# Staging the last weight through three buffers, and the front of a seven-product stage, in a three-layer kernel on one core

## The chip, the cores and the metric

The kernel runs on one core of one Trainium2 chip. The metric is the device time of one execution in microseconds; the median of three executions before the change is 565.75 us (564.25 to 565.76). Five engines matter, each with a queue of its own that is worked off in order: TensorE (PE), VectorE (DVE), ScalarE (ACT), GpSimd (POOL) and SyncE (SP), which here only starts transfers.

## What is computed

```python
x = attention(q, k, v)        # 2 x 8 heads, 768 positions, head size 64: a window of +-15
                              # positions and one summary (max of k, mean of v) per 32 positions
x = x.transpose(0, 2, 1, 3).reshape(1536, 512)
a, b = x @ w1, x @ w2         # 512 -> 1024
x = ((a * b) @ w3) @ w_out    # 1024 -> 1024 -> 512
h = x @ w_in                  # 512 -> 2048
g = h * clip(h + 3, 0, 6) / 6
out = g @ moe2_w_out          # 2048 -> 512
```

The weights are float64 and reach the chip as pairs of 32-bit words. All large products are made in float32 quality: each operand is held as a rounded part and a remainder, and a product of two such operands is three matmuls.

## The kernel before, in words

The 1536 rows are three blocks of 512. A slot of the arena holds one 128 x 512 tile as its two parts (1024 words a partition). PE first multiplies w3 and w_out into one weight W', then for each block forms a and b from w1 and w2 (16 tiles, the middle weights), the gated tile a * b, and accumulates it against W' over eight tiles (`acc1`, 12 matmuls of 128 x 512 each). Attention is cut into twelve tiles of 128 positions; the first four are block 0's. Its steps and the middle weights' conversion lie between PE's matmuls.

For blocks 1 and 2 the products with six of the eight w1/w2 pairs are made by a seven-product scheme: sums and differences of pieces of x (`sums_of_x`, once) and of pieces of the weights (for each unit) are multiplied, so that seven half products (`half1`, six matmuls each) do the work of eight. There are six units, (q, w) with q = 1, 2, 3 and w = 0 for w1, 1 for w2. Products 1 and 2 take raw operands alone; 5, 6, 7, 4 and 3 take sums. Banks 4 to 7 of PSUM hold them; `copy1` takes a bank to SBUF by ACT, `add1` adds a bank to such a copy by DVE. Product 7 goes onto a bank that product 4 writes further, so that 4 waits for the copy of 7. Between the two stand up to two fills: `to_fill` puts half accumulations of a gated tile on a list, `filled1` takes them from it. Gated tiles of block 2 go to DRAM (`gm`) and are fetched behind the stage. The second layer pair runs by the same scheme over blocks 0 and 1 (`w_in_group`, `w_out_group`, `half_product`), the output product of these blocks stands last.

The last weight (moe2_w_out, 16 tiles of 512 KB) has a way of its own, `convert_out`: SP loads a tile into a staging buffer `raw`, ACT widens the high words (L286), ACT or DVE shifts the low words (L292, L297), DVE joins both (L301), ACT rounds (L310), POOL subtracts (L313), all in `raw` and a second buffer `c`, and `spill` writes the 512 KB to DRAM as `wo`, from where they come back later. There are four buffers `raw` and four `c` in this part of the kernel; the last weight uses two of the first and four of the second. The other two `raw` lend their halves to the seven-product stage as temporaries.

The order on each engine isn't written by hand: every operation is entered in a graph with an engine, an assumed duration and its data. `schedule` walks through assumed time and gives each engine, of the operations ready by then, the one that is due first. Due times come from PE operations, and from `cap` where one is given, and are carried back to whatever feeds them, less durations and an assumed latency (LAT; LAT_SP for SP). `slack` puts off the users of an operation, `begin` is its earliest time. So the planner's numbers fix an order; the chip then runs this order with real waits. A 512 KB load of the last weight is planned at 1311 ns + LAT_SP + HOLD before its first user is ready, its spill at 1300 ns + LAT_SP + HOLD/2.

Buffers are handed out in the order in which operations are entered. The last weight is entered behind the middle weights, so that its loads wait for the last users of these in the same buffer.

Of the kernel before, what the change touches and what calls it, by code (L numbers as in the profile page):

```python
# [161 lines left out]
LO_DVE = [2, 9, 11, 14, 17, 18, 22, 26, 28, 29, 30, 31, 32, 36, 39, 42, 44, 45, 47]  # L162
L3_ACT = [1, 2, 3, 4, 5, 6, 7, 8, 10, 11, 12, 15, 17, 18, 20, 22, 23]
DUE_FF = 31.69
AHEAD, BEHIND = -27.19, -170.09
SUMS_AT, SUMS_DUE = 3, 0.61
# [12 lines left out]
OUT_AT, OUT_STEP = 104.69, 5.24


def build(tc, qd, kw, vw, kt, vt, consts, wp_in, w12_in, w2_in, out):
# [518 lines left out]
    with tc.manual_schedule():  # L701
# [190 lines left out]

        for q in range(NFC // 2):
            if q in DIRECT:
                continue
            for w in range(2):
                ws = [w12(2 * q + w), w12(2 * (q + 4) + w)] + [A_MID + 2 + 2 * (n_unit % 2) + i for i in range(2)]
                (a, ka), (b, kb) = fw
                whole_of(due, a, ka, ws[0], both(ws[0]), W_ENG[2])
                whole_of(due, b, kb, ws[1], both(ws[1]), W_ENG[3])  # L900
                in_place(due, a, ka, b, kb, (
                    (("b", 1), ("b", 0), ALU.add, ("b", 1)),
                    (("b", 0), ("a", 0), ALU.subtract, ("b", 0)),
                    (("a", 0), ("b", 1), ALU.subtract, ("a", 0)),
                    (("a", 1), ("a", 1), ALU.subtract, ("a", 0)),
                ), W_ENG[4])
                for i in range(2):
                    hi_lo_slot(due, fw[i][0], fw[i][1], ws[2 + i], W_ENG[i])
                bA, bB, bC = (4 + (3 * n_unit + i) % 4 for i in range(3))
                n_unit += 1  # L910
                o = fc if w else fa
                half1(ws, 1, bA, True)
                copy1(bA, fb[0])
                half1(ws, 5, bC, True)
                half1(ws, 6, bA, False)
                copy1(bA, fb[1])
                half1(ws, 2, bB, True)
                add1(bB, fb[0], o[0])
                if w:
                    product1(fa[0], o[0], o[0], G_ENG[0])  # L920
                    g11 = use1(o[0], q)
                half1(ws, 7, bA, False)
                copy1(bA, fb[2])
                filled1(2)
                add1(bC, fb[2], o[1])
                half1(ws, 4, bA, False)
                half1(ws, 3, bC, False)
                if w:
                    product1(fa[1], o[1], o[1], G_ENG[1])
                    hold1(o[1], q + 4)  # L930
                    t = fa[3]
                    g.op("dve", 690, due, lambda b=bA, t=t: nc.vector.tensor_tensor(
                        out=t[0](), in0=bank[b], in1=t[0](), op=ALU.mult), [("bank", bA)], [t[1]])
                    g21 = use1(t, q + 4)
                else:
                    copy1(bA, fa[3])
                add1(bC, fb[1], o[2])
                if w:
                    product1(fa[2], o[2], o[2], G_ENG[2])
                    hold1(o[2], q)  # L940
                    to_fill(q, g11)
                    to_fill(q + 4, g21)
# [375 lines left out]
```

## Time and profile before

| | us |
|---|---|
| median of the executions | 565.75 |
| the profiled execution | 566.23 |
| its span, first to last instruction | 564.5 |
| PE busy | 526.8 |
| DVE busy | 421.2 |
| ACT busy | 317.5 |
| POOL busy | 289.6 |
| mean granted TensorE clock, share of full speed | 0.986 |

The profile gives each engine's busy time, and for each instruction what ended the idle time before it. A share is an average over stages; what a stage is worth is read from PE's gaps in it and from what released them. A PE that is busy at half the clock shows no gap.

### The profile page before, as it was taken

To read this page: it belongs to the slowest core of one execution; us is meant where nothing else is said; L and a number is where in the kernel's file an instruction comes from. 1 tells how busy PE (TensorE), PEld (TensorE's weight loads), DVE (VectorE), ACT (ScalarE), POOL (GpSimd) and SP (SyncE) were. 2 spreads that over 40 slices of the span, in tenths; PEclk is the share of its full clock that TensorE was granted. 3 is DMA by queue.
4 is the path that set the end of the run, shared out by engine and by line. 5 is a ranking of instruction groups with operands and counts; after the bars stand their busy time and mean duration, and the time that the engine had idled before them with its cause. 6 is when DMAs were issued, how large, how long until landed. Compare 5 with 4: busy or idle time off the path is not lost.

```text
span 564.5 us, 8632 instructions
## 1 busy us (share of the span) xinstructions
PE 526.8 (93%) x3076; PEld 429.2 (76%) x3076; DVE 421.2 (75%) x549; ACT 317.5 (56%) x547; POOL 289.6 (51%) x239
## 2 busy tenths in 40 slices
PE   1499989989998999998999999999999998999997
PEld 0478778778776887776888888888888886888875
DVE  5879868787866789877689878787666558689650
ACT  1888786575444754636455676656654455643530
POOL 0667546866444401112364578887776553644440
PEclk9999999999998999997999999999999998999999
DMA  8999877773664831563586356674436779877631
GB/s 320 353 341 338 231 246 243 233 228 96 200 228 172 303 120 62 183 181 122 187 288 226 113 161 215 221 261 163 150 135 194 246 242 366 275 240 226 192 108 74
DMA packets 57971, 119.73 MB, mean 212 GB/s; under 512 B 5176, under 2 KB 26680, under 8 KB 57928
## 3 DMA queue, kind: packets, MB, share of 16 engines
q1 hardware_dynamic: 57928, 119.18, 63.7%
q8 instruction: 24, 0.39, 0.3%
q14 instruction: 19, 0.16, 0.1%
HBM read 88.46 MB, written 30.41 MB: 211 GB/s over the span
## 4 chain that ended last, share of the span: by engine, by line
PE 79%; DMA 10%; ACT 4%; DVE 3%; POOL 2%; issue 1%; SPq 1%; ACTq 0%; POOLq 0%; DVEq 0%
PE bank L357 74%; DMA raw<-in_w_dram 4%; PE bank L493 2%; PE bank L554 2%; DMA qst<-in_q_dram 1%; PE bank L539 1%; DMA kres<-in_kt_dram 1%; DMA arena<-wo 1%; DMA ws<-arena 1%; DMA wo<-raw 1%; ACT c L286 1%; ACT arena L310 1%; DVE c L301 1%; ACT raw L292 1%; POOL late_f L797 1%
## 5 line engine op out<-in xcount | busy, mean ns | idle before, releaser
L357 PE MATMUL bank<-arena,w 128*128 128x512 f32 x1008 | 236.3, 392 | 2.9 <-ACT late_f L1027 2.9
L357 PEld LDWEIGHTS bank<-arena,w 128*128 128x128 f32 x1008 | 189.5, 189 | 44.2 <-ACT late_f L1027 4.4
L357 PE MATMUL bank<-arena 128*128 128x512 f32 x888 | 220.1, 399 | 0.0
L357 PEld LDWEIGHTS bank<-arena 128*128 128x128 f32 x888 | 167.4, 191 | 36.1 <-issue 0.5
L313 POOL TENSOR_TENSOR raw<-c,raw 128x512 fp32r<-128x512 f32 x16 | 20.9, 1312 | 78.9 <-ACT raw L310 65.7
L313 POOL TENSOR_TENSOR w<-c,w 128x512 fp32r<-128x512 f32 x29 | 41.0, 1416 | 38.7 <-ACT w L310 38.0
L310 ACT ACTIVATE arena<-late_f 128x512 fp32r<-128x512 f32 x64 | 39.4, 628 | 35.1 <-DVE late_f L797 19.0
L301 DVE SCALAR_TENSOR_TENSOR c<-c,raw 128x512 uint32<-128x512 uint32 x48 | 43.8, 918 | 17.2 <-ACT raw L292 16.9
L286 ACT ACTIVATE c<-raw 128x512 f32<-128x512 f32 x48 | 32.0, 669 | 42.4 <-DMA raw<-in_w_dram 32.9
L313 DVE TENSOR_TENSOR arena<-late_f,arena 128x512 fp32r<-128x512 f32 x44 | 38.3, 879 | 11.5 <-ACT arena L310 11.4
L313 POOL TENSOR_TENSOR arena<-late_f,arena 128x512 fp32r<-128x512 f32 x20 | 28.7, 1435 | 32.5 <-ACT arena L310 27.7
L292 ACT ACTIVATE raw<-raw 128x512 uint32<-128x512 uint32 (+1 forms) x67 | 43.2, 648 | 0.0
L357 PE MATMUL bank<-arena,mid 128*128 128x512 f32 x144 | 37.1, 401 | 3.6 <-ACT ta L865 3.6
L998 POOL TENSOR_TENSOR late_f<-arena 128x512 f32<-128x512 f32 x16 | 26.0, 1626 | 27.7 <-DMA arena<-wo 12.9
L313 POOL TENSOR_TENSOR arena<-c,arena 128x512 fp32r<-128x512 f32 (+1 forms) x22 | 28.1, 1286 | 19.0 <-ACT arena L310 16.5
L357 PEld LDWEIGHTS bank<-arena,mid 128*128 128x128 f32 x144 | 27.6, 193 | 10.2 <-ACT ta L865 4.5
L1046 DVE SCALAR_TENSOR_TENSOR late_f<-ta,late_f 128x512 f32<-128x512 f32 x24 | 29.0, 1210 | 5.3 <-ACT ta L1043 5.1
L529 POOL TENSOR_TENSOR sc<-sc,st 128x960 f32<-128x960 f32 x12 | 22.6, 1884 | 14.8 <-DVE st L525 14.8
L797 DVE TENSOR_TENSOR late_f<-arena,late_f 128x512 f32<-128x512 f32 x24 | 25.0, 1068 | 6.6 <-DMA arena<-gj 5.3
L310 ACT ACTIVATE w<-c 128x512 fp32r<-128x512 f32 x40 | 24.7, 626 | 8.0 <-DVE c L301 5.2
L519 POOL TENSOR_TENSOR sc<-sc,st 128x960 f32<-128x960 f32 x12 | 22.4, 1864 | 8.3 <-DVE st L517 8.3
L1060 ACT ACTIVATE ta<-bank,three 128x512 f32<-128x512 f32 x16 | 11.0, 688 | 26.1 <-PE bank L357 26.1
(103 smaller groups left out, 716.5 us busy)
## 6 DMA issues: line engine op xcount, KB each, us to landing
raw<-in_w_dram SPq DMA_DIRECT2D x48, 512.0 KB, 4.4
raw<-in_wp_dram SPq DMA_DIRECT2D x22, 512.0 KB, 6.0
wo<-raw SPq DMA_DIRECT2D x16, 512.0 KB, 3.0
arena<-wo SPq DMA_DIRECT2D x16, 512.0 KB, 3.7
ws<-arena SPq DMA_DIRECT2D x16, 512.0 KB, 3.4
w<-ws SPq DMA_DIRECT2D x32, 256.0 KB, 3.5
arena<-gj SPq DMA_DIRECT2D x24, 256.0 KB, 5.4
w<-wo SPq DMA_DIRECT2D x24, 256.0 KB, 3.5
```

Source lines behind the costliest of these rows:

```text
L286: lambda uf=uf, wf=wf: nc.scalar.activation(out=uf, in_=wf[:, :, 1], func=AF.Prelu, scale=2.0**-112, alpha=-(2.0**32)),
L292: lambda lw=lw: nc.scalar.activation(out=lw, in_=lw, func=AF.Copy, scale=2.0**-29 * (1 - eps), bias=7.5 * eps - 0.5),
L301: lambda ci=ci, ui=ui, lw=lw: nc.vector.scalar_tensor_tensor(out=ci, in0=ui, scalar=3, in1=lw, op0=ALU.logical_shift_left, op1=ALU.bitwise ...
L310: lambda: nc.scalar.activation(out=hi(), in_=src(), func=AF.Copy), keys, khi)
L313: lambda: e.tensor_tensor(out=lo(), in0=src(), in1=hi().bitcast(F32), op=ALU.subtract),
L357: nc.tensor.matmul(out=out_ap, lhsT=lhs(a), rhs=rhs(c), start=start and n == 0, stop=stop and n == 3 * len(terms) - 1, skip_group_check=skip,)
L493: nc.tensor.matmul(out=bank[bk[x]][o : o + D, p * NK + c : p * NK + c + rhs.shape[-1]], lhsT=qs[pr, x, p, :], rhs=rhs, start=True, stop=True,)
L519: lambda: nc.gpsimd.tensor_tensor(out=s8, in0=s8, in1=wide(0), op=ALU.subtract), [("st", i2)], skeys)
L529: lambda: nc.gpsimd.tensor_tensor(out=s8, in0=s8, in1=wide(1), op=ALU.mult), [("st", i2)], skeys)
L797: lambda: e.tensor_tensor(out=out(), in0=a(), in1=b(), op=op), [ka, kb], [ko], True)
L998: lambda i=i, s=s: nc.gpsimd.tensor_tensor(out=tmps[6 + i], in0=f32s(s, 0)(), in1=f32s(s, 1)(), op=ALU.add), both(s), [k])
L1046: lambda: nc.vector.scalar_tensor_tensor(out=dst(), in0=t, scalar=6.0, in1=h(), op0=ALU.min, op1=ALU.mult),
```

## The change

It does six things.
1. `convert_out` takes three `raw` buffers in place of two, and two `c` in place of four. The temporaries of the seven-product stage thus lose raw 2: `sums_of_x` uses six places for eight (two of them twice), products and outputs are written onto their own inputs, and the sums of a weight pair lie in c2 and c3.
2. The first two units are split: sums, products 1 and 2 of unit (1, 0), two fills, the same of unit (1, 1), and only then products 5, 6, 7, 4, 3 of both. The first gated tile of a pair goes to the fills as soon as product 2 is there.
3. Behind the stage the eight gated tiles of block 2 are fetched into the second half of the slot in which they are used as an operand, and rounded there, the first two into slots of middle weights, the others into the ring of three; before they were fetched into temporaries.
4. The eight whole-tile adds in `sums_of_x` over blocks 0 and 1 go from POOL to DVE (X2_ENG).
5. LAT_SP grows from 1716 to 2657 ns, HOLD from 1168 to 4066. The last weight's conversions may begin from 56.7 us in steps of 6.14, with a pause of 36.5 behind the ninth, where before they began at 104.7 in steps of 5.24; their caps lie 12.3 behind the start where before they lay 14.7 ahead.
6. Other due times and three lists of which engine does a step are new.

```diff
-LAT_SP = 1716.09
+LAT_SP = 2656.58
-DUE_W = ((77.78, -6.43), (102.28, 1.95))
-DUE_K, DUE_V, DUE_ROWS = 181.53, -74.16, -60.66
-DUE_Q = (307.31, 50.25)
+DUE_W = ((92.0, -6.43), (102.28, 1.95))
+DUE_K, DUE_V, DUE_ROWS = 192.51, -53.65, -55.94
+DUE_Q = (243.64, 53.46)
...
+X2_ENG = ['dve', 'dve', 'dve', 'dve', 'dve', 'dve', 'dve', 'dve']
-HOLD = 1168.47
-SUMS_LATER = 23929.09
-OUT_LATER = 23001.01
-IN_AT = (15, 16)
+HOLD = 4065.6
+SUMS_LATER = 27418.12
+OUT_LATER = 34008.61
+IN_AT = (14, 16)
-OUT_CAP = -14.65
-OUT_AT, OUT_STEP = 104.69, 5.24
+OUT_CAP, OUT_PAUSE, OUT_N = 12.29, 36.53, 9
+OUT_AT, OUT_STEP = 56.69, 6.14
...
-        r, c = take("raw", n_raw), take("c", N_C)
+        r, c = take("raw", n_raw), take("c", n_c)
...
-        r, c, parts = to_f32(due, src, n_raw=2, slack=HOLD, begin=begin)
+        r, c, parts = to_f32(due, src, n_raw=3, slack=HOLD, begin=begin, n_c=2)
...
-        m_temps = [temp(i) for i in range(4)] + halves
+        m_temps = [temp(0), halves[0], temp(1), halves[1], temp(2), temp(3), temp(0), temp(1)]
+        spare = [(lambda c=c: cs[c].bitcast(F32), ("c", c)) for c in (2, 3)]
...
+        for w in range(2):
+            q, ws = units[w][0], slots_of[units[w]]
+            c0 = tatg[3] if w else fb[0]
+            sums_of_w(ws)
+            half1(ws, 1, 4 + 2 * w, True)
+            copy1(4 + 2 * w, c0)
+            half1(ws, 2, 5 + 2 * w, True)
+            first_output(q, w, 5 + 2 * w, c0, c0 if w else fa[0])
+            filled1(2)
+        for w in range(2):
+            q, ws = units[w][0], slots_of[units[w]]
+            bA, bC = 4 + 2 * w, 5 + 2 * w
+            half1(ws, 5, bC, True)
+            half1(ws, 6, bA, False)
+            copy1(bA, fb[1])
+            other_outputs(q, w, ws, bA, bC)
...
-            t = temp(8 + n)
+            gs = A_W1 + 4 + n if n < 2 else g_slot()
             d = spilled["gm", i]
-            g.op("sp", 700, due, lambda t=t, d=d: nc.sync.dma_start(out=t[0](), in_=d), [("gm", i)], [t[1]])
-            gs = use1(t, i)
+            g.op("sp", 700, due, lambda gs=gs, d=d: nc.sync.dma_start(out=f32s(gs, 1)(), in_=d), [("gm", i)],
+                 [("t", gs, 1)])
+            g.op("act", 630, due, lambda gs=gs: nc.scalar.activation(
+                out=slot(gs)[:, 0, :], in_=f32s(gs, 1)(), func=AF.Copy), [("t", gs, 1)], [("t", gs, 0)])
+            tensors(due, lambda gs=gs: slot(gs)[:, 1, :], f32s(gs, 1), f32s(gs, 0), ALU.subtract,
+                    ("t", gs, 1), ("t", gs, 0), ("t", gs, 1), "dve")
...
-        sums_of_x(due, (0, 1), tslot, [temp(i) for i in range(8)], both, ["pool"] * 4 + ["dve"] * 4)
+        sums_of_x(due, (0, 1), tslot, [temp(i) for i in range(8)], both, X2_ENG)
...
             convert_out(due + n // 2 * OUT_LATER, w2_in[NFC2 + tile_of(n)], ("wo", n),
-                        begin=(OUT_AT + OUT_STEP * n) * us)
+                        begin=(OUT_AT + OUT_STEP * n + OUT_PAUSE * (n >= OUT_N)) * us)
```

## Rows read from the trace of the kernel before

**Rows 1.** The page's part 1: busy us, share of the span, instructions.
```profile
PE 526.8 (93%) x3076; PEld 429.2 (76%) x3076; DVE 421.2 (75%) x549; ACT 317.5 (56%) x547; POOL 289.6 (51%) x239
```
**Rows 2.** Timeline of PE at its gaps: start, us, instruction, [idle before and releaser].
```profile
72.78 1.15 PE L554 MATMUL bank<-pt,vall 120*64 120x64 f32 x32 [1.80 <-ACT pt L546]
...
124.54 1.05 PE L493 MATMUL bank<-kall,qst 64*64 64x120 f32 x32 [1.50 <-DVE arena L571]
...
159.23 1.15 PE L554 MATMUL bank<-pt,vall 120*64 120x64 f32 x32 [1.14 <-ACT pt L546]
...
172.82 1.25 PE L554 MATMUL bank<-pt,vall 120*64 120x64 f32 x32 [1.88 <-ACT pt L546]
...
230.68 3.01 PE L357 MATMUL bank<-arena,mid 128*128 128x512 f32 x12 [0.69 <-ACT ta L865]
...
256.35 2.93 PE L357 MATMUL bank<-arena,mid 128*128 128x512 f32 x6 [2.93 <-ACT ta L865]
...
471.16 7.09 PE L357 MATMUL bank<-arena,w 128*128 128x512 f32 x24 [2.67 <-ACT late_f L1027]
```
**Rows 3.** Busy time by window, the start: window, length, engines, PEclk, DMA share, GB/s.
```profile
0.00:26.30 26.30, 6.01 (x132) 5.01 (x132) 17.25 (x23) 12.73 (x25) 8.65 (x16) 1.00 0.95 336
```
**Rows 4.** The same view behind three of the gaps.
```profile
172.80:177.30 4.50, 4.48 (x40) 3.70 (x41) 3.75 (x6) 2.73 (x5) 1.79 (x1) 0.62 0.69 201
256.30:262.50 6.20, 6.15 (x15) 4.81 (x16) 5.17 (x8) 2.20 (x4) 2.33 (x2) 0.50 0.64 182
471.10:474.10 3.00, 2.94 (x7) 2.36 (x8) 2.96 (x5) 1.25 (x3) 1.27 (x2) 0.50 1.07 388
```
**Rows 5.** Timeline of ACT ahead of two of the gaps.
```profile
171.10 0.66 ACT L286 ACTIVATE c<-raw 128x512 f32<-128x512 f32 x1 [3.52 <-DMA raw<-in_w_dram]
...
172.18 0.58 ACT L546 ACTIVATE pt<-bank 120x512 f32<-120x512 f32 x1
...
254.09 0.66 ACT L286 ACTIVATE c<-raw 128x512 f32<-128x512 f32 x1 [4.33 <-DMA raw<-in_w_dram]
...
255.72 0.58 ACT L865 ACTIVATE ta<-bank 128x512 f32<-128x512 f32 x1
```
**Rows 6.** ACT's waits from 120 to 300 us: total us, times, longest.
```profile
ACT c L286 <- DMA raw<-in_w_dram: 23.8, 10, 4.3
```
**Rows 7.** DMA issues: count, KB each, median us from issue to landing.
```profile
raw<-in_w_dram SPq DMA_DIRECT2D x48, 512.0 KB, 4.4
...
late_f<-gm SPq DMA_DIRECT2D x8, 256.0 KB, 5.2
```
**Rows 8.** Timeline of ACT ahead of the gap at 124.54.
```profile
119.25 0.67 ACT L286 ACTIVATE c<-raw 128x512 f32<-128x512 f32 x1 [2.31 <-DMA raw<-in_w_dram]
```
**Rows 9.** Timeline of ACT ahead of the gap at 471.16.
```profile
468.35 0.63 ACT L310 ACTIVATE arena<-late_f 128x512 fp32r<-128x512 f32 x1 [3.68 <-DMA ws<-arena]
```
**Rows 10.** Busy time by window at the head of the stage of units.
```profile
212.00:228.00 16.00, 15.31 (x68) 12.36 (x67) 15.49 (x26) 6.40 (x13) 2.58 (x2) 1.00 0.27 103
```
**Rows 11.** Timeline of PE behind the stage of units.
```profile
296.76 19.28 PE L357 MATMUL bank<-arena 128*128 128x512 f32 x84
```
**Rows 12.** POOL's eight adds; DVE's groups from 291 to 304, then 304 to 318.
```profile
291.50 11.84 POOL L809 TENSOR_TENSOR late_f<-arena 128x512 f32<-128x512 f32 x8 [0.78 <-PE bank L357]
...
L797 DVE TENSOR_TENSOR arena<-late_f,arena 128x512 fp32r<-128x512 f32 x4 | 6.7, 1734 | 0.0
...
L797 DVE TENSOR_TENSOR arena<-late_f,arena 128x512 fp32r<-128x512 f32 x4 | 2.8, 690 | 1.1 <-ACT arena L888 1.1
```
**Rows 13.** Timeline of SP: the end of the middle weights' loads, then two loads into one buffer.
```profile
121.26 0.92 SPq L258 DMA_DIRECT2D raw<-in_w_dram  x2
...
153.85 0.35 SPq L258 DMA_DIRECT2D raw<-in_w_dram  x1
...
167.41 0.35 SPq L258 DMA_DIRECT2D raw<-in_w_dram  x1
```
**Rows 14.** Busy time by window from 110 to 165 us.
```profile
110.00:165.00 55.00, 52.35 (x469) 41.60 (x471) 43.35 (x56) 31.37 (x54) 30.96 (x22) 1.00 0.60 194
```

More of the change, by code (lines that the diff above doesn't have):

```diff
@@ L154, in schedule @@
         return sorted(order)
-DUE_W = ((77.78, -6.43), (102.28, 1.95))
-DUE_K, DUE_V, DUE_ROWS = 181.53, -74.16, -60.66
-DUE_Q = (307.31, 50.25)
+DUE_W = ((92.0, -6.43), (102.28, 1.95))
+DUE_K, DUE_V, DUE_ROWS = 192.51, -53.65, -55.94
+DUE_Q = (243.64, 53.46)
 V_AT = 1
[L162 to L166, printed above, removed]
+LO_DVE = [9, 14, 17, 18, 20, 22, 26, 27, 28, 29, 30, 31, 34, 37, 39, 40, 42, 44, 45]
+L3_ACT = [1, 2, 3, 4, 5, 6, 7, 9, 10, 11, 13, 14, 15, 17, 18, 20, 21, 22]
+DUE_FF = 30.52
+AHEAD, BEHIND = -25.17, -177.18
+SUMS_AT, SUMS_DUE = 2, 0.46
 POOL_MAX = ()
 DIRECT = (0, 4)
-LATER, LATER0 = 2.88, -2.39
+LATER, LATER0 = 3.04, -2.43
+X2_ENG = ['dve', 'dve', 'dve', 'dve', 'dve', 'dve', 'dve', 'dve']
 X_ENG = ("dve",) * 8
-W_ENG = ("dve", "dve", "dve", "dve", "dve")
+W_ENG = ['dve', 'dve', 'dve', 'dve', 'dve']
 G_ENG = ("dve", "dve", "dve")
-HOLD = 1168.47
-SUMS_LATER = 23929.09
-OUT_LATER = 23001.01
-IN_AT = (15, 16)
+HOLD = 4065.6
+SUMS_LATER = 27418.12
+OUT_LATER = 34008.61
+IN_AT = (14, 16)
 LAST_ORDER = (0, 1, 4, 5, 2, 3, 6, 7)
-OUT_CAP = -14.65
-OUT_AT, OUT_STEP = 104.69, 5.24
+OUT_CAP, OUT_PAUSE, OUT_N = 12.29, 36.53, 9
+OUT_AT, OUT_STEP = 56.69, 6.14
 def build(tc, qd, kw, vw, kt, vt, consts, wp_in, w12_in, w2_in, out):
@@ L259, in load, with to_f32 @@
              slack=slack, begin=begin)
-    def to_f32(due, src, pieces=1, banks=None, n_raw=N_RAW, slack=0, begin=0):
-        r, c = take("raw", n_raw), take("c", N_C)
+    def to_f32(due, src, pieces=1, banks=None, n_raw=N_RAW, slack=0, begin=0, n_c=N_C):
+        r, c = take("raw", n_raw), take("c", n_c)
         kr, kc = ("raw", r), ("c", c)
@@ L839, in slot_keys @@
             return both(s) + [k for k in x_keys(x) if k[1] == s]
-        halves = [half_raw(r, h) for r in (2, 3) for h in range(2)]
-        g.op("late", 1, 0, lambda: None, (), [("raw", 2), ("raw", 3)] + [k for _, k in halves])
+        halves = [half_raw(3, h) for h in range(2)]
+        g.op("late", 1, 0, lambda: None, (), [("raw", 3)] + [k for _, k in halves])
         tatg = [(lambda i=i: ta[i], ("ta", i)) for i in range(2)] + [(lambda i=i: tg[i], ("tg", i)) for i in range(2)]
-        m_temps = [temp(i) for i in range(4)] + halves
+        m_temps = [temp(0), halves[0], temp(1), halves[1], temp(2), temp(3), temp(0), temp(1)]
+        spare = [(lambda c=c: cs[c].bitcast(F32), ("c", c)) for c in (2, 3)]
         XT = {1: [A_X, A_X + 1], 2: [A_X + 2, A_X + 3], 3: [A_X + 2 * NPAIR, A_X + 2 * NPAIR + 1], 4: [A_MID, A_MID + 1]}
@@ L851, in build @@
         }
-        fa, fb, fc = m_temps[:4], tatg[:3], [tatg[3]] + halves[:2]
-        fw = halves[2:]
+        fa, fb, fw = [temp(i) for i in range(4)], tatg[:3], spare
         n_unit = 0
@@ L891, in use1 @@
             return gs
[L893 to L942, printed above, removed]
@@ new lines, in sums_of_w @@
+        def sums_of_w(ws):
+            (a, ka), (b, kb) = fw
+            whole_of(due, a, ka, ws[0], both(ws[0]), W_ENG[2])
+            whole_of(due, b, kb, ws[1], both(ws[1]), W_ENG[3])
+            in_place(due, a, ka, b, kb, (
+                (("b", 1), ("b", 0), ALU.add, ("b", 1)),
+                (("b", 0), ("a", 0), ALU.subtract, ("b", 0)),
+                (("a", 0), ("b", 1), ALU.subtract, ("a", 0)),
+                (("a", 1), ("a", 1), ALU.subtract, ("a", 0)),
+            ), W_ENG[4])
+            for i in range(2):
+                hi_lo_slot(due, fw[i][0], fw[i][1], ws[2 + i], W_ENG[i])
@@ new lines, in first_output, with other_outputs @@
+        def first_output(q, w, b, c0, o):
+            add1(b, c0, o)
+            if w:
+                product1(fa[0], o, fa[0], G_ENG[0])
+                to_fill(q, use1(fa[0], q))
+        def other_outputs(q, w, ws, bA, bC):
+            o1, o2 = (fb[2], fb[1]) if w else (fa[1], fa[2])
+            half1(ws, 7, bA, False)
+            copy1(bA, fb[2])
+            filled1(2)
+            add1(bC, fb[2], o1)
+            half1(ws, 4, bA, False)
+            half1(ws, 3, bC, False)
+            t = fa[3]
+            if w:
+                product1(fa[1], o1, fa[1], G_ENG[1])
+                hold1(fa[1], q + 4)
+                g.op("dve", 690, due, lambda: nc.vector.tensor_tensor(
+                    out=t[0](), in0=bank[bA], in1=t[0](), op=ALU.mult), [("bank", bA)], [t[1]])
+                to_fill(q + 4, use1(t, q + 4))
+            else:
+                copy1(bA, t)
+            add1(bC, fb[1], o2)
+            if w:
+                product1(fa[2], o2, fa[2], G_ENG[2])
+                hold1(fa[2], q)
@@ new lines, in build @@
+        units = [(q, w) for q in range(NFC // 2) if q not in DIRECT for w in range(2)]
+        slots_of = {
+            (q, w): [w12(2 * q + w), w12(2 * (q + 4) + w)] + [A_MID + 2 + 2 * (n % 2) + i for i in range(2)]
+            for n, (q, w) in enumerate(units)
+        }
+        for w in range(2):
[6 more added lines that the diff above has]
+            first_output(q, w, 5 + 2 * w, c0, c0 if w else fa[0])
+            filled1(2)
@@ new lines, in build @@
+        for w in range(2):
[5 more added lines that the diff above has]
+            other_outputs(q, w, ws, bA, bC)
+        for n, (q, w) in enumerate(units[2:]):
+            ws = slots_of[q, w]
+            sums_of_w(ws)
+            bA, bB, bC = (4 + (3 * n + i) % 4 for i in range(3))
+            half1(ws, 1, bA, True)
+            copy1(bA, fb[0])
+            half1(ws, 5, bC, True)
+            half1(ws, 6, bA, False)
+            copy1(bA, fb[1])
+            half1(ws, 2, bB, True)
+            first_output(q, w, bB, fb[0], fb[0] if w else fa[0])
+            other_outputs(q, w, ws, bA, bC)
@@ L943, in build @@
         filled1(99)
         x2_out(due, 1)
-        g.op("late", 1, 0, lambda: None, (), [("raw", 2), ("raw", 3)] + [k for _, k in halves])
+        g.op("late", 1, 0, lambda: None, (), [("raw", 3)] + [k for _, k in halves])
         g.op("late", 1, 0, lambda: open_tiles(pools.pop(), "late", "right", A_LATE, N_LATE, N_TMP), (),
```

## The prediction

> **What bounds the kernel now.** I read the page's busy shares first: TensorE (PE) is busy 526.8 of 564.5 us [rows 1]. The change neither adds nor drops a matmul, so at most the other 37.7 us and what the clock loses can be won. Next the timeline of PE for its gaps, as each line names its releaser [rows 2]. Up to 26.3 us it was busy 6.01 [rows 3]: 20.3 us of the 37.7 are the start. Then come 1.80 (at 72.78), 1.50 (124.54), 1.14 (159.23), 1.88 (172.82), twice 0.69 in the stage of six units (the second at 230.68), 2.93 (256.35) and 2.67 (471.16): 13.3 us in eight gaps; what is left, 4.1, is the tail behind the last matmul and crumbs. Third, the clock: PE kept 2.4 GHz behind the gap of 1.80, but behind three others it ran partly or wholly at 1.2 GHz [rows 4]: 4.5 us at 0.62, 6.2 at 0.50, 3.0 at 0.50. At 1 - 0.62 and 1 - 0.50 of these stretches that is 1.7 + 3.1 + 1.5 = 6.3 us. Mid-kernel loss: 13.3 + 6.3 = 19.6 us.
>
> Fourth, what the releasers of these gaps had been doing. ACT works in its order. At 171.10 its widening step L286 starts after 3.52 us of waiting for the load of a last weight; the attention copy L546, which PE needs, stands behind it and starts at 172.18. At 254.09 the same: 4.33 us of waiting, and the copy L865 for which PE has been idle starts at 255.72 [rows 5]. A third pair of this kind ends the gap at 159.23. From 120 to 300 us ACT waits so for 23.8 us, ten times [rows 6]. So a plan that expected these loads too early costs 1.14 + 1.88 + 1.7 + 2.93 + 3.1 = 10.8 us.
>
> **The change part by part.** *Waits on transfers.* In the planner's arithmetic a 512 KB load takes 1.31 us to issue plus LAT_SP, and HOLD more before L286 counts as ready: 1.31 + 1.72 + 1.17 = 4.20 us before, 1.31 + 2.66 + 4.07 = 8.03 after. A spill is 3.60 before and 5.99 after. The chip lands such a load in 4.4 us in the median [rows 7]. What is late is the turn of a buffer: load, some 4.0 of arithmetic (three ACT steps near 0.65, one of DVE, one of POOL) and spill are 11.8 us in the plan, but two loads into one buffer start at 153.85 and 167.41, 13.6 us apart [rows 13]; the loads that alternate with them use the other buffer. So each turn slips 1.8 us, and ACT, whose other work follows PE, reaches L286 ahead of the load. After, a turn is planned at 18.0 us: slower than the chip's 13.6, so the slip turns into slack, and L286 stands 3.84 us later against its load, while the waits were 4.33 at the longest. Of 10.8 us I take 10.3 away, less the 0.5 by which the longest exceeds 3.84. The third buffer keeps the pace: 18.0/3 = 6.0 us a tile, 11.8/2 = 5.9 before; with two buffers the new plan would need 9.0. SP issues as many DMAs as before; a load or spill that waits on SP still holds what follows there (attention's q and v loads up to 196 us).
>
> The gap at 124.54 lies behind a wait of 2.31 us for a load of the middle weights [rows 8]; those get only LAT_SP's 0.94: 0.94/2.31 x 1.50 = 0.6 us.
>
> The gap at 471.16 lies behind an ACT step that waited 3.68 us for a spill's landing [rows 9]; these spills get 2.39 more. If all of it arrives, 0.3 of the 2.67 remains, and with the 1.5 of the clock 3.9 us are won; if the transfers merely queue, nothing. I take 2.4, nearer the upper end, as the wait is of the kind that a later place in the order removes.
>
> *Raw-operand products in front.* Products 1 and 2 of the first two units need neither sums of x nor of weights, and four fills stand between: eight times six matmuls, 8 x 1.38 = 11.0 us (twelve take 2.75, below), where before product 5, which needs both sums, came second. VectorE (DVE) is busy 15.49 of 16 us there [rows 10], but no gap of before waits for a sum: both 0.69s are copies of a bank to SBUF that ACT makes late. Now the four early fills leave the second unit without any between product 7 and its copy: one such 0.69 may return. Zero, between -1.4 and +1.4.
>
> *Temporaries in place.* No instruction more. The sums of a weight pair move from halves of raw 3 to staging buffers c2 and c3; the first middle-weight group behind the stage (w_in_group) takes just these and must wait for the last pair's sums. Its cover is the seven accumulations of 19.28 us [rows 11] that PE does before it needs more than the first operand of that group. Zero; with the cover gone, a wait of a transfer, 4.4.
>
> *Gated tiles into operand slots.* Eight fetches land in the slot's second half, ACT rounds it and DVE subtracts in place. The first two slots are free early; the others are a ring of three, so fetch n waits for accumulation n - 3. One accumulation is 19.28/7 = 2.75 us, so the fetch has 5.5 us. It takes 5.2 to land [rows 7], 0.63 on ACT, as L310's rounding [rows 9], and 0.69 on DVE [rows 12], and some 0.4 of issue and hops: 6.9. Short by 1.4 once: the next fetches start from earlier accumulations and stay just behind. 0 if the planner puts a product of the next stage between, which needs only raw operands, 1.4 + 1.7 of clock if not; nearer zero, 0.6.
>
> *Adds from GpSimd (POOL) to DVE (X2_ENG).* POOL loses eight adds that took it 11.84 us; DVE gains 8 x 0.69 = 5.5. But four DVE operations beside them took 1.73 against 0.69, 4.2 us [rows 12]. Nearly even; PE has no gap there.
>
> *New dues.* Dues without a PE operation (SUMS_LATER, OUT_LATER, DUE_K, DUE_V, BEHIND) have no effect in this planner: it takes dues from PE operations and caps only. The rest is a new order on each engine, the start's included. Conversions of the last weight may begin from 56.7 in the plan, but its buffers belong to the middle weights until those are loaded, at 121.26 here [rows 13]. An order has gaps of its own: I charge one more like 172.82's with its clock, 1.88 + 1.7 = 3.6, at three chances in four: 2.7; bounds -3.3 (the 1.80 gone and a start 1.5 earlier) and +7.2 (two such).
>
> **Sum.** 10.3 + 0.6 + 2.4 - 0.6 - 2.7 = 10.0 us. The profiled execution took 566.23 (span 564.5), the median is 565.75; taken from the median, 555.8.
>
> **A rule of the skill against the row.** The row gives 4.4 us for a load. The Trainium skill, DMA: Bandwidth & Descriptors, section Anatomy of one DMA, fits 2.0 us plus bytes at 436 GB/s, on GpSimd's path, not the one used here: an estimate from that page of 3.2 us. By it the plan's 4.20 was long enough already, the longer hold would add nothing, and the second rival's half would be all. The trace disagrees on the landing (4.4).
>
> **The rivals.**
> *1. Slower: the last weight pushes in ahead of attention.* OUT_CAP gives the first nine conversions earlier dues (69 to 118 in the plan, against 90 to 132). Each is three ACT steps, 2.0 us, one or two DVE and a POOL step. From 110 to 165 DVE is busy 43.35 of 55 us and ACT 31.37 [rows 14]. If they stand before the copies of attention, each of the tiles behind 110 us gets a gap like 172.82's, 3.6 us. Beyond three tiles (10.0/3.6) the gain is gone; five cost 18: 565.75 - 10.0 + 18 = 573.8. For it: three gaps of before are attention's. Against: those were waits for transfers, not too much work on ACT.
> *2. Only half of it.* L286's wait at 171.10 begins 0.2 us after the load's issue at 167.41, and the load lands in 3.7, within the old plan's 4.20. What is late is the issue, and if it is late for more than the turn of two buffers (SP's order, POOL's step), the third buffer and the hold take only half of the 10.3: 565.75 - 5.2 - 0.6 - 2.4 + 3.3 = 560.9. Against: the planned turn of 18.0 leaves 4.4 us over the chip's 13.6.
> *3. No difference: the change doesn't do what it says.* The buffers are held by the middle weights, the longer hold pushes the sixteen conversions later, and the gap at 256.35 with its clock (6.0) merely moves, the last one (2.4) too: 10.0 - 6.0 - 2.4 = 1.6, 564.2. For it: at 254.09 the conversions of before are still going on in the stage of units [rows 5]. Against: the new plan's pace of 6.0 is above what the chip can do with three buffers, 13.6/3 = 4.5.
>
> **How the numbers follow.** Forecast 0.62, second rival 0.13, third 0.13, first 0.12. A measurement of this kernel tells 0.3% from no change: 564.1 to 567.4 is the same. So faster 0.62 + 0.13 = 0.75, same 0.13, slower 0.12. Likeliest 555.8. The range: the low end is all of the 19.6 us without new gaps, 546, where I stop at 547.5, as 10.8 of it at most is argued from this cause; the high end takes in the third rival and a small part of the first, 568.0.
>
> **What would show each step.** Of the hold: ACT's total wait for loads at L286 falls from 23.8 us to under 5, the gaps at 159, 172 and 256 go and with them the half clock. Of the ring: a PE gap behind an ACT step that waits for a gated tile. Of the front: no DVE-released PE gap at the head of the stage of units, and a copy-released one in the second. Of POOL's adds: DVE's L797 back at 0.69. Of the first rival: PE gaps before L554, released by L546, with no transfer before it. The prediction is wrong if ACT no longer waits for loads and PE idles as long as before, or if the start takes several us more or less than 26.3.

## The result, and the profile after

The changed kernel takes 558.12 us in the median of four executions (555.32 to 558.73), the kernel before 565.41 beside it: 0.9865 of the time, 95% interval 0.9828 to 0.9901. That is 7.3 us less; 10.0 were forecast, and the time lies inside the range. Run again beside the experiments, the kernel gave 0.9869 (0.9821 to 0.9916); its median of 555.61 is 8.0 us under the 563.66 beside it.

| | before | after |
|---|---|---|
| profiled execution, us | 566.23 | 558.23 |
| its span | 564.5 | 556.4 |
| PE busy | 526.8 | 523.9 |
| PE idle in the span | 37.7 | 32.5 |
| mean granted TensorE clock | 0.986 | 0.996 |

The span is 8.1 us shorter: 5.2 of idle time and 2.9 of busy time, with as many matmuls. The busy time follows the clock, but not alone: two forms of attention's small matmuls (L554 and L539, now L555 and L540) were busy 14.2 and 13.8 us, 0.6 more than before together. Part 1 of the page of the changed kernel, to be read beside [rows 1]:

```profile
PE 523.9 (94%) x3076; PEld 426.3 (77%) x3076; DVE 424.7 (76%) x556; ACT 316.8 (57%) x548; POOL 272.7 (49%) x231
```

The timeline of PE in the changed kernel at its gaps, as in [rows 2]. In the changed kernel the same statements stand one line further down (L286 is L287, L865 is L866), behind the stage of units 29 lines (L1027 is L1056).

```profile
27.97 1.96 PE L540 MATMUL bank<-con,sc 128*120 128x128 f32 x8 [6.46 <-POOL sc L530]
...
64.34 7.79 PE L358 MATMUL bank<-arena 128*128 128x512 f32 x33 [0.97 <-DVE arena L697]
...
244.78 4.61 PE L358 MATMUL bank<-arena,mid 128*128 128x512 f32 x12 [2.08 <-DVE mid_f L870]
...
277.30 1.65 PE L358 MATMUL bank<-arena,mid 128*128 128x512 f32 x6 [0.69 <-ACT ta L866]
279.64 1.65 PE L358 MATMUL bank<-mid,w 128*128 128x512 f32 x6 [0.69 <-ACT tg L866]
...
462.66 5.78 PE L358 MATMUL bank<-arena,w 128*128 128x512 f32 x24 [0.49 <-ACT late_f L1056]
...
518.10 1.66 PE L358 MATMUL bank<-arena,w 128*128 128x512 f32 x6 [0.71 <-ACT late_f L1056]
520.73 31.89 PE L358 MATMUL bank<-arena,w 128*128 128x512 f32 x138 [0.97 <-ACT late_f L1056]
```

All three gaps between 100 and 200 us are gone. The 2.93 at 256.35 has no successor with its releaser; a gap of 2.08 with another releaser stands at 244.78. The 2.67 near 470 is 0.49. New are 0.71 and 0.97 near the end. The windows of the changed kernel (window, length, busy time of PE, PEld, DVE, ACT, POOL, PEclk, DMA share, GB/s) show the start, the stage of attention, and the stretch behind 244.78:

```profile
0.00:28.00 28.00, 6.01 (x133) 5.03 (x133) 18.26 (x23) 13.10 (x26) 9.99 (x17) 1.00 0.98 349
100.00:200.00 100.00, 100.00 (x842) 79.96 (x841) 88.50 (x114) 63.40 (x108) 51.28 (x45) 1.00 0.67 222
244.70:249.50 4.80, 4.72 (x14) 3.74 (x15) 2.85 (x7) 2.23 (x4) 0.00 (x0) 0.64 0.59 201
```

The same two long windows of the kernel before:

```profile
0.00:28.00 28.00, 7.67 (x141) 6.68 (x141) 18.92 (x26) 13.59 (x26) 10.35 (x17) 1.00 0.95 336
100.00:200.00 100.00, 95.48 (x818) 76.36 (x817) 74.82 (x103) 55.80 (x95) 53.78 (x45) 0.98 0.63 210
```

So 4.5 us were won in the stage of attention (95.48 to 100.00, clock 0.98 to 1.00), and 1.66 were lost by 28 us. What ACT waited for from 100 to 300 us (total us, times, longest), after; before it was 28.5 us in 13 waits:

```profile
ACT c L287 <- DMA raw<-in_w_dram: 16.1, 8, 4.2
```

From 120 to 300 us, the stretch of [rows 6], it is the same 16.1. The waits did not vanish, but in this execution none of PE's gaps stands behind one of them. In attention L287 still waits 3.48 us at 195.86, and later 3.12 and 4.19:

```profile
195.86 0.68 ACT L287 ACTIVATE c<-raw 128x512 f32<-128x512 f32 x1 [3.48 <-DMA raw<-in_w_dram]
...
237.09 0.68 ACT L287 ACTIVATE c<-raw 128x512 f32<-128x512 f32 x1 [3.12 <-DMA raw<-in_w_dram]
...
245.29 0.67 ACT L287 ACTIVATE c<-raw 128x512 f32<-128x512 f32 x1 [4.19 <-DMA raw<-in_w_dram]
```

The gap at 244.78 has a cause of its own, which the timelines of DVE and of SP show. The adding step L870 waits 3.51 us until a spilled tile has landed in `gm`, because the tile is now held in place, in the memory into which L870 writes next:

```profile
235.12 0.69 DVE L798 TENSOR_TENSOR mid_f<-mid_f,tg 128x512 f32<-128x512 f32 x1
...
244.03 0.69 DVE L870 TENSOR_TENSOR mid_f<-bank,tg 128x512 f32<-128x512 f32 x1 [3.51 <-DMA gm<-mid_f]
```
```profile
231.13 0.97 SPq L328 DMA_DIRECT2D wo<-raw  x1
238.36 0.33 SPq L259 DMA_DIRECT2D raw<-in_w_dram  x1
238.74 0.90 SPq L885 DMA_DIRECT2D gm<-mid_f  x2
```

The tile was complete at 235.12 + 0.69 = 235.8. Its spill was issued only at 238.74, behind a load of the last weight. SP had come to that load at 231.13 + 0.97 = 232.1 and waited 6.2 us there, until the spill out of the buffer that the load fills had landed (`wo<-raw`).

### The profile page after: what moved, and what is told of

Same layout as the page of the kernel before. It is cut to its first block, busy times and chain, and to the rows that moved or that the text cites. A ratio compares the mean times of both kernels' runs of the same rounds, so it can differ in the third digit from the quotient of the medians.

```text
span 556.4 us, 8619 instructions
## 1 busy us (share of the span) xinstructions
PE 523.9 (94%) x3076; PEld 426.3 (77%) x3076; DVE 424.7 (76%) x556; ACT 316.8 (57%) x548; POOL 272.7 (49%) x231
## 4 chain that ended last, share of the span: by engine, by line
PE 86%; DMA 6%; DVE 4%; ACT 1%; issue 1%; SPq 1%; POOL 0%; ACTq 0%; DVEq 0%; POOLq 0%
PE bank L358 79%; PE bank L494 2%; PE bank L555 2%; PE bank L540 2%; DVE late_f L798 2%; DMA kres<-in_kt_dram 1%; DMA qst<-in_q_dram 1%; DMA raw<-in_w_dram 1%; DMA arena<-gj 1%; DMA gm<-mid_f 1%; DVE arena L314 1%; SPq L259 1%; ACT arena L311 0%; DVE c L1212 0%; POOL sc L530 0%
## 5 line engine op out<-in xcount | busy, mean ns | idle before, releaser
L358 PE MATMUL bank<-arena 128*128 128x512 f32 x888 | 217.5, 395 | 1.0 <-DVE arena L697 1.0
L358 PEld LDWEIGHTS bank<-arena 128*128 128x128 f32 x888 | 165.1, 189 | 36.6 <-DVE arena L697 1.4
L302 DVE SCALAR_TENSOR_TENSOR c<-c,raw 128x512 uint32<-128x512 uint32 x48 | 47.5, 997 | 6.3 <-ACT raw L293 5.1
L314 POOL TENSOR_TENSOR arena<-late_f,arena 128x512 fp32r<-128x512 f32 x20 | 29.3, 1468 | 35.8 <-ACT arena L311 28.5
L1027 POOL TENSOR_TENSOR late_f<-arena 128x512 f32<-128x512 f32 x16 | 22.9, 1434 | 47.7 <-DVE late_f L798 21.4
L287 ACT ACTIVATE c<-raw 128x512 f32<-128x512 f32 x48 | 31.8, 664 | 20.8 <-DMA raw<-in_w_dram 17.3
L314 POOL TENSOR_TENSOR arena<-c,arena 128x512 fp32r<-128x512 f32 (+1 forms) x22 | 26.6, 1222 | 20.0 <-ACT arena L311 19.2
L798 DVE TENSOR_TENSOR late_f<-arena,late_f 128x512 f32<-128x512 f32 x24 | 25.3, 1081 | 11.1 <-DMA arena<-gj 8.2
L530 POOL TENSOR_TENSOR sc<-sc,st 128x960 f32<-128x960 f32 x12 | 23.0, 1920 | 5.9 <-DVE st L526 5.2
L1092 DVE SCALAR_TENSOR_TENSOR tg<-ta,bank 128x512 f32<-128x512 f32 x16 | 11.0, 687 | 17.7 <-ACT ta L1089 17.7
```

Source lines behind the costliest of these rows:

```text
L287: lambda uf=uf, wf=wf: nc.scalar.activation(out=uf, in_=wf[:, :, 1], func=AF.Prelu, scale=2.0**-112, alpha=-(2.0**32)),
L302: lambda ci=ci, ui=ui, lw=lw: nc.vector.scalar_tensor_tensor(out=ci, in0=ui, scalar=3, in1=lw, op0=ALU.logical_shift_left, op1=ALU.bitwise ...
L314: lambda: e.tensor_tensor(out=lo(), in0=src(), in1=hi().bitcast(F32), op=ALU.subtract),
L358: nc.tensor.matmul(out=out_ap, lhsT=lhs(a), rhs=rhs(c), start=start and n == 0, stop=stop and n == 3 * len(terms) - 1, skip_group_check=skip,)
L530: lambda: nc.gpsimd.tensor_tensor(out=s8, in0=s8, in1=wide(1), op=ALU.mult), [("st", i2)], skeys)
L798: lambda: e.tensor_tensor(out=out(), in0=a(), in1=b(), op=op), [ka, kb], [ko], True)
```

## The experiments

Each was compared with the kernel before on its own chip (563.5 to 563.75 us there). Differences to the changed kernel are differences of ratios times 563.6, against its 0.9869; by the medians they come out up to 1.5 us apart. "After" is the changed kernel.

**The two waits put back.** After, with the plan's two transfer times of before.

```diff
-LAT_SP = 2656.58
+LAT_SP = 1716.09
-HOLD = 4065.6
+HOLD = 1168.47
```


> The changed kernel with the planner's old transfer times (LAT_SP 1716, HOLD 1168), three buffers kept. Theory 1 (the plan's longer transfer times took the gaps away): ACT's waits for loads of the last weight between 100 and 300 us rise from 16.1 to over 22 us, at least two PE gaps over 1 us come back between 100 and 200 us, 563 to 567 us. Theory 2 (the third buffer alone did it): no PE gap over 1 us there, 556 to 560 us.

566.48 us, ratio 1.0055 (1.0030 to 1.0081): 10.5 us over the changed kernel, and slower than before. Theory 1 held. The profile is of the slowest of seven executions (570.80). ACT's waits, a PE gap, and ACT ahead of it:

```profile
ACT c L287 <- DMA raw<-in_w_dram: 32.3, 13, 4.5
```
```profile
196.43 2.64 PE L358 MATMUL bank<-arena 128*128 128x512 f32 x6 [2.62 <-DVE pt L545]
```
```profile
186.52 0.67 ACT L287 ACTIVATE c<-raw 128x512 f32<-128x512 f32 x1 [3.50 <-DMA raw<-in_w_dram]
187.09 0.99 ACT L521 ACTIVATE sc<-sc 128x960 f32<-128x960 f32 x1
```

The softmax step L521 stands behind L287's wait of 3.50 us, DVE's and POOL's work on it follows, and the copy L545 at its end is what PE idles for. PE is busy 95.12 of 100 us in attention again, at a clock of 0.98, and a gap of 3.42 stands at 474.38. Without the two numbers nothing of the gain is left.

**The two waits alone.** The kernel before, with the new values of LAT_SP and HOLD and nothing else.

```diff
-LAT_SP = 1716.09
+LAT_SP = 2656.58
-HOLD = 1168.47
+HOLD = 4065.6
```


> The kernel before with LAT_SP 2657 and HOLD 4066 alone. Theory 1: the gaps at 159, 172 and 256 us go, ACT's waits for these loads fall from 23.8 to under 16 us, 556 to 561 us, as much as the whole change. Theory 2: within 3 us of before, 563 to 568 us.

569.21 us, ratio 1.0097 (1.0065 to 1.0128), slower than either theory had it. The waits nearly vanish all the same:

```profile
ACT c L286 <- DMA raw<-in_w_dram: 6.1, 6, 1.8
```
```profile
60.44 6.69 PE L357 MATMUL bank<-arena 128*128 128x512 f32 x21 [2.81 <-DVE arena L696]
...
194.98 0.98 PE L357 MATMUL bank<-arena 128*128 128x512 f32 x3 [1.56 <-DVE arena L636]
...
217.26 0.50 PE L357 MATMUL bank<-arena,mid 128*128 128x512 f32 x1 [2.75 <-ACT mid L310]
```

The gaps at 159, 172 and 256 are gone, as theory 1 wants, but PE idles elsewhere: 6.6 us from 30 to 100 and 8.1 from 200 to 300. The last weight's conversions, which the longer hold pushes back, can't explain the first stretch: the plan lets none begin before 104.7. What made these gaps wasn't followed further. So the long waits are needed for the gain and don't give it alone. ACT's total wait didn't rank the kernels: 6.1 us here at 569, 16.1 in the changed kernel at 558.

**Only the hold.** After, with the old LAT_SP and the new HOLD.

```diff
-LAT_SP = 2656.58
+LAT_SP = 1716.09
```


> The changed kernel with the old LAT_SP (1716) and the long HOLD (4066). Theory A (HOLD is what frees attention, LAT_SP is what costs the start): no PE gap over 1 us between 100 and 200 us, first transposes near 26.4, 553 to 557 us. Theory B (LAT_SP carries it, as it applies to all loads): gaps of 1 to 3 us return between 100 and 200 us, 560 to 566 us.

562.02 us, ratio 0.9975 (0.9955 to 0.9995): 6.0 over the changed kernel, 4.5 under the one with both short. Theory A has the gaps right (none over 0.87 us from 100 to 200) and the start, theory B the time. PE is busy 98.08 us in attention. Its timeline, then ACT's:

```profile
17.53 0.71 PE L494 MATMUL bank<-kres,qst 64*64 64x96 f32 x8 [1.49 <-DMA qst<-in_q_dram]
26.68 1.96 PE L540 MATMUL bank<-con,sc 128*120 128x128 f32 x8 [6.69 <-POOL sc L530]
...
279.67 2.93 PE L358 MATMUL bank<-mid,w 128*128 128x512 f32 x6 [2.99 <-ACT tg L866]
```
```profile
278.48 0.66 ACT L287 ACTIVATE c<-raw 128x512 f32<-128x512 f32 x1 [2.46 <-DMA raw<-in_w_dram]
279.04 0.58 ACT L866 ACTIVATE tg<-bank 128x512 f32<-128x512 f32 x1
```

The pattern of [rows 5] is back in the last unit, and so is a gap of 2.25 near 467. HOLD clears most of attention, LAT_SP the rest. LAT_SP also makes the start later: without it PE's first transposes (L540) are at 26.68, with it at 27.97. LAT_SP alone made long was not run.

**Two staging buffers.** After, with `convert_out` taking two `raw`.

```diff
-        r, c, parts = to_f32(due, src, n_raw=3, slack=HOLD, begin=begin, n_c=2)
+        r, c, parts = to_f32(due, src, n_raw=2, slack=HOLD, begin=begin, n_c=2)
```


> The changed kernel with two staging buffers for the last weight, the long transfer times kept. Theory 1: no PE gap over 1 us between 100 and 200 us, as the plan is slower than the chip; the sixteen spills end later than in the changed kernel (there at 283 us), near 300, 557 to 562 us. Theory 2: gaps like those of before (1.1 to 1.9 us) return, 562 to 567 us.

557.49 us, ratio 0.9908 (0.9879 to 0.9937), 2.2 over the changed kernel with intervals that overlap. Attention has one gap, of 0.87; near the end of the units one of the old kind is left, and the gap at 244 is not there:

```profile
275.06 2.93 PE L358 MATMUL bank<-arena,mid 128*128 128x512 f32 x6 [2.47 <-ACT ta L866]
```

Theory 1 held in gaps and time. A gain from the third buffer isn't shown, and most of the gain is had without it. The last spill goes out at 288.92, against 283.06 in the changed kernel.

**The held tiles apart.** After; the gated tiles that wait for their spill go to two halves that are free then, not in place.

```diff
-                product1(fa[1], o1, fa[1], G_ENG[1])
-                hold1(fa[1], q + 4)
+                h1 = halves[0] if q < 3 else fa[1]
+                product1(fa[1], o1, h1, G_ENG[1])
+                hold1(h1, q + 4)
...
```


> The changed kernel with the two gated tiles that go to DRAM written to the free halves of raw 3 in the first two pairs, and not onto their own input. Theory (the output in place made a new wait: DVE's add stood 3.51 us for the spill of the tile to land, PE 2.08 behind it at 244.78 and then at 1.2 GHz): gap and half clock go, 553.5 to 556 us. Rival (the gap comes from SP, which issued the two spills 3 us late behind a load that waited for its buffer): the gap stays within 1 us of its size somewhere in the stage, 557 to 559 us.

555.59 us, ratio 0.9871 (0.9841 to 0.9902). The gap of 2.08 is gone, and two smaller ones stand in its place, 0.37 at 252.85 and this one:

```profile
246.50 1.66 PE L358 MATMUL bank<-arena 128*128 128x512 f32 x6 [0.94 <-ACT mid_f L866]
```

The two spills went out as late as before (238.89 and 239.80), but L870 no longer waited for one. So the wait for the tile's memory made the gap, and SP's late issue made it long. The new gap of 0.94 is of the kind of [rows 5]: L866, at 245.87, stands behind a wait of 3.50 us by L287. Taking the old gap away moves no time that can be told, partly because the changed kernel beside it lost little to that gap:

**The changed kernel again.** No edit.

> The changed kernel itself, on the chip of the runs beside it, as their base. Ratio to the kernel before as first measured, 0.983 to 0.990.

555.61 us, the ratio in the expected range. The gap stands where it stood, but the clock holds (second fence: a window with PE's busy time alone):

```profile
244.19 3.01 PE L358 MATMUL bank<-arena,mid 128*128 128x512 f32 x12 [2.10 <-DVE mid_f L870]
```
```profile
240.00:260.00 20.00, 17.91 (x79) 1.00 0.57 201
```

PE is busy 522.1 us at a mean clock of 1.000, against 523.9 at 0.996 in the first profile.

**Gated tiles by way of temporaries.** After, with the eight fetches into `late_f` as before the change.

```diff
-            gs = A_W1 + 4 + n if n < 2 else g_slot()
+            t = temp(8 + n)
...
+            g.op("sp", 700, due, lambda t=t, d=d: nc.sync.dma_start(out=t[0](), in_=d), [("gm", i)], [t[1]])
+            gs = use1(t, i)
```


> The changed kernel with the eight gated tiles fetched into temporaries and split from there, as before the change. Theory (fetching into operand slots is covered either way): no PE gap over 0.7 us from 285 to 315 us, within 1.5 us of the changed kernel. Rival (the early fetch into slots of middle weights covers the emptying of the banks): a gap of 1 to 3 us behind the stage of units.

562.48 us, ratio 0.9988 (0.9967 to 1.0009): 6.7 over the changed kernel. The rival is nearer, but its gap was to be 1 to 3 us. PE has one large gap, and SP shows why:

```profile
291.84 8.43 PE L358 MATMUL bank<-arena 128*128 128x512 f32 x26 [6.17 <-ACT arena L889]
```
```profile
282.84 0.38 SPq L885 DMA_DIRECT2D gm<-mid_f  x1
283.33 0.90 SPq L259 DMA_DIRECT2D raw<-in_w_dram  x2
287.14 3.66 SPq L979 DMA_DIRECT2D late_f<-gm  x8
```

The late temporaries share memory with those of the stage, so the first fetch waits for the last held tile's spill: issued at 282.84, landed before 287.14. Fetches into operand slots need none of that memory and start at 229.75 in the changed kernel. There is no PE gap near 244 in this run: the spills of the held tiles went out from 235.98, and L870 waited 0.93 us for one of them.

**The front undone.** After, with all six units in one plain loop.

```diff
-        for w in range(2):
-            q, ws = units[w][0], slots_of[units[w]]
...
-        for n, (q, w) in enumerate(units[2:]):
+        for n, (q, w) in enumerate(units):
```


> The changed kernel with the first two units in the plain order of the other four (product 5 second), all else kept. Theory (the front matters, as in the run with long waits alone PE stood 2.75 and 0.79 us at the head of the stage for rounded sums): one or two gaps of together 2 to 4 us between 200 and 225 us, released by the rounding or the subtraction of a sum, 2 to 5 us slower than the changed kernel. Rival (the front is worth nothing, as the prediction had it): no such gap, within 1.5 us of the changed kernel.

557.03 us, ratio 0.9900 (0.9867 to 0.9933), 1.7 over the changed kernel with overlapping intervals. That is nearer to the rival. At the head of the stage two gaps of 0.75 and 0.69 are released by copies, none by a sum.

**The adds back on POOL.** After, with X2_ENG such that POOL does the eight whole-tile adds.

```diff
-X2_ENG = ['dve', 'dve', 'dve', 'dve', 'dve', 'dve', 'dve', 'dve']
+X2_ENG = ['pool', 'pool', 'pool', 'pool', 'dve', 'dve', 'dve', 'dve']
```


> The changed kernel with the eight whole-tile adds of the second scheme back on GpSimd. Theory (moving them is even): within 1.5 us of the changed kernel's 555.6, DVE's two-input operations beside them back at 1.7 us. Rival (DVE is the tighter one, 88.5 of 100 us from 100 to 200): 1 to 3 us faster than the changed kernel.

560.74 us, ratio 0.9932 (0.9905 to 0.9959): 3.6 over the changed kernel by the ratios, 5.1 by the medians, where one theory had it even and the other faster. The two ran on different chips, and the intervals overlap by 0.0011, so the size is uncertain. DVE's groups from 280 to 310 us with the adds on POOL (busy us, mean ns):

```profile
L798 DVE TENSOR_TENSOR arena<-arena 128x512 fp32r<-128x512 f32 x5 | 6.9, 1387 | 1.7 <-ACT arena L981 1.7
L798 DVE TENSOR_TENSOR late_f<-late_f,late_f 128x512 f32<-128x512 f32 x6 | 6.5, 1135 | 0.0
```

The same view of the changed kernel:

```profile
L798 DVE TENSOR_TENSOR late_f<-late_f,late_f 128x512 f32<-128x512 f32 x8 | 5.2, 687 | 0.0
L798 DVE TENSOR_TENSOR arena<-arena 128x512 fp32r<-128x512 f32 x5 | 3.4, 690 | 1.3 <-ACT arena L981 1.3
```

And PE with the adds on POOL, which has no gap there in the changed kernel (busy 50.00 of 50 us from 280 to 330):

```profile
313.57 1.67 PE L358 MATMUL bank<-arena,w 128*128 128x512 f32 x6 [1.18 <-ACT late_f L1056]
316.25 7.09 PE L358 MATMUL bank<-arena,w 128*128 128x512 f32 x30 [1.00 <-ACT late_f L1056]
```

**The dues of the start as before.** After, with three due times of before (the first of DUE_W, DUE_ROWS, DUE_Q).

```diff
-DUE_W = ((92.0, -6.43), (102.28, 1.95))
-DUE_K, DUE_V, DUE_ROWS = 192.51, -53.65, -55.94
-DUE_Q = (243.64, 53.46)
+DUE_W = ((77.78, -6.43), (102.28, 1.95))
+DUE_K, DUE_V, DUE_ROWS = 192.51, -53.65, -60.66
+DUE_Q = (307.31, 50.25)
```


> The changed kernel with the old dues of W', of the first attention tiles and of the summary rows. Theory A (these dues cost the start 1.6 us but keep 30 to 100 us free of gaps): the first transposes near 26.5 in place of 27.97, but gaps of together 2 to 5 us between 30 and 100 us as in the run with long waits alone, 0 to 4 us slower. Theory B (the later start is plain loss): the gaps between 30 and 100 stay at 1.0, 1 to 2 us faster.

556.46 us, ratio 0.9882 (0.9829 to 0.9936); the first transposes at 27.89. Neither theory held: these due times do nothing that can be measured.

**The second q load pulled forward**, alone and together with the held tiles apart. In the changed kernel SP issues it behind six loads of 512 KB; before, it went out at 9.41, behind four:

```profile
6.14 5.00 SPq L259 DMA_DIRECT2D raw<-in_wp_dram  x6
12.32 0.33 SPq L259 DMA_DIRECT2D qst<-in_q_dram  x1
```
```diff
-        load(due - 5 * us, lambda: qs, qd[u], P * 2048, [("qs", i2)])
+        g.op("sp", 655, due, lambda: nc.sync.dma_start(out=qs, in_=qd[u]), (), [("qs", i2)], cap=(u - 11) * us if u < 2 else None)
```


> The changed kernel with the load of the second attention tile's q given a cap, so that SP issues it ahead of the first loads of w3 and w_out. Theory (the start is 1.6 us later because LAT_SP put that load behind six of those, issued at 12.32 in place of 9.41): its scores start before 16 us, the first transposes at 25 to 26.5, 552.5 to 554.5 us. Rival (the start is bound by the loads of w3 and w_out, which now come 0.7 us later each): first transposes earlier, but PE idles as long up to 40 us, 555 to 557 us.

> Both repairs: the second q load ahead, and the held tiles apart as in the run of that name (555.6). Theory: the gain at the start adds, 552 to 554.5 us. Rival (each repair only reshuffles the order and other gaps take the place): 555 to 557 us.

559.69 us (0.9933, 0.9911 to 0.9956) and 557.85 (0.9900, 0.9878 to 0.9922), both above what either theory had. The second scores came 2 us earlier, at 16.97, but PE then idled 7.76 us for POOL's L530, and the first transposes stood at 27.62. So that load alone doesn't bound the start, and the shifted order left gaps of 1.22 at 192.86 and 1.13 at 276.76. What it is of LAT_SP's effect that holds the start back by 1.3 us stays open. The new places of the last weight's conversions (OUT_CAP, OUT_AT, OUT_STEP) and the lists of engines were not undone by themselves; so which parts of the change the two long waits need is known only in part. No kernel tried here was faster than the changed one by more than the intervals tell; the held tiles apart are level with it.

## Why the prediction was right, and where its terms were off

**Cause and sign.** The step that carried the sum held: ACT's waits in its own order, ahead of what PE needs. Undoing the two numbers costs 10.5 us and brings the chain back. By 1.31 + LAT_SP + HOLD the forecast called it one cause with one size; the run with HOLD alone shows two parts, 4.5 by HOLD and 6.0 by LAT_SP on top. The forecast didn't see that the two numbers alone, in the old order, make the kernel slower.

| term | forecast | by the two profiles |
|---|---|---|
| gaps at 159, 172, 256, idle | +5.5 | +5.95, all three gone |
| their clock | +4.8 | +4.2 |
| gap at 124.54 | +0.6 | +1.50 |
| gap at 471, with its clock | +2.4 | +2.18 + 1.3 |
| ring of gated tiles | -0.6 | 0, no PE gap from 300 to 450 us |
| temporaries in place | 0 | -3.6 |
| new order, the rest | -2.7 | -2.5 |
| sum | 10.0 | 9.0; the spans differ by 8.1 |

The forecast's 10.3 is split here into 5.95 + 4.8 less its 0.5. Most of the 0.9 that the sum has over the spans is the 0.6 us of busy time in attention's small matmuls, which no term names. That the sum came within 2 us is in part luck: the gains at 124.54 and 471 came out 2.0 above their terms, and the loss by the temporaries in place 3.6 above its zero.

**The clock terms.** They were made as one minus the clock times the stretch. Counted by matmuls they are somewhat smaller. One takes 19.28/84 = 0.23 us at 2.4 GHz [rows 11]. Behind 256.3, 15 of them were busy 6.15 us [rows 4]: 6.15 - 3.45 = 2.7 lost, not 3.1. Behind 471.1 it is 2.94 - 7 x 0.23 = 1.3, not 1.5. Behind 172.8 stand 32 small matmuls that took 1.25 us, against 1.15 at 72.78 [rows 2], and then 18 large ones, which the changed kernel does in 4.42 us at the full clock (first fence: before; second: after):

```profile
174.00 5.85 PE L357 MATMUL bank<-arena 128*128 128x512 f32 x18
```
```profile
94.16 4.42 PE L358 MATMUL bank<-arena 128*128 128x512 f32 x18
```

So 1.5 were lost there, not 1.7. Forecast 6.3, measured 5.5.

**Temporaries in place: the term that failed most.** This was priced at zero with c2 and c3 as the only new wait. The new wait was another one: the held tile's memory stays taken until its spill has landed, and SP's order puts that spill behind a load that is itself held up. The forecast followed SP's queue for the conversions' loads, not for this spill. It cost 2.08 us of idle time and, by the 14 matmuls behind it, 4.72 - 3.2 = 1.5 of clock in the first profile. That this lies within the 4.4 given for lost cover is luck, as the 4.4 was for another wait.

**New order.** Charged at 2.7, the rest of it cost 2.5: the start 1.66 and the end 0.71 + 0.97, less 1.80 - 0.97 = 0.83 at 64.34. Of the start 1.3 came with LAT_SP, which the forecast applied to the loads and spills of the weights and not to the order of the first loads, although every transfer from SP is planned with it.

**The gap at 124.54.** It is gone, but the reason given, LAT_SP's 0.94 us, isn't shown: neither run with the old LAT_SP in the changed kernel has a PE gap there. Another part of the change is enough to take it away.

**The third buffer.** It was to keep the pace, 6.0 us a tile against 9.0 with two. With two the kernel lost nothing that can be told.

**Gated tiles into slots.** Taken as a small cost. The cost was zero, and with the held tiles in place the old way costs 6.7 us. An edit that pays for another's side effect can't be priced against the kernel before alone.

**Adds to DVE.** Called even: POOL's 11.84 us against DVE's 5.5 less 4.2. In the run they are worth some 3.6 to 5.1, with intervals that overlap. The kernel before had no PE gap behind POOL's adds (busy 150.00 of 150 us from 300 to 450), as the forecast said; in the changed kernel PE idles behind them, at 313.57 and 316.25, and not behind the adds on DVE. The balance of busy times didn't tell that. Whether it is the 8 x 1.5 us on POOL coming late or DVE slowed beside them, the run doesn't separate. The Trainium skill, SBUF — State Buffer, section Who interferes with whom, says that a DVE instruction with two SBUF inputs contends with a GpSimd instruction that reads SBUF. The trace agrees: L798 took 1387 and 1135 ns in the mean beside POOL's adds, 690 and 687 without.

**The front.** Zero with 1.4 either way; 1.7 in its favour, with intervals that overlap, so not told from zero. Copy-released gaps at the head came without it, not with it.

**ACT's waits under 5 us.** A miss: 16.1. The forecast's view was the total, and the kernel before with the long waits had 6.1 and was slower. What decides is which instruction stands behind the wait: with the held tiles apart, one of 3.50 us made a PE gap, and in the changed kernel one of 4.19 did not.

**The rivals.** The first: no gap in attention, so no. The second, half the gain: no; all three gaps went, and putting the old values back costs 10.5. By the estimate of 3.2 us from the Trainium skill, DMA: Bandwidth & Descriptors, section Anatomy of one DMA, the longer hold would have added nothing; the runs speak against that, with 4.5 us for HOLD. The third said the gap at 256 would merely move. A gap 11.6 us earlier does stand there, but it is released by another step for another reason, and attention's and the late gap were won all the same.

## What to carry to other kernels

In this kernel an engine that works in order turned a late transfer into a stall for everything behind it (3.52 us of waiting at L286, then the copy L546 for which PE idled). In the changed order it paid to plan a transfer with more than its time to landing: 8.03 us in place of 4.20, where the landing takes 4.4 and the turn of a buffer 13.6. Only these two values of each number were run, so the best one isn't known. Change such a number together with what the order depends on, and look for the new place of the idle time; a smaller total of waits shows nothing. When a temporary is written in place, list the transfers that still read it and the queue in which they stand.

## What was not expected of the hardware

The same gap in the same program had two outcomes for the clock. With 2.08 us of idle time at 244.78 the stretch behind it ran at 0.64; with 2.10 us at 244.19, in another execution, 1.00. In the kernel before the clock was 1.00 from 72.7 to 78 us, behind a gap of 1.80, and 0.62 behind one of 1.88 [rows 2, 4]. The four executions of the first comparison had mean clocks of 0.996, 0.995, 1.000 and 0.996, and took 558.23, 558.73, 555.32 and 558.0 us: the one at 1.000 is 10.1 us under the median before. How much of a gain of this kind is seen depends in part on the clock behind gaps near 2 us, which no row here foretells.
